# A decode step of attention with a gated feed-forward: the gate's weights in nine DMAs, V's last tiles in pieces, the last head of wo in 21 parts

## Chip, cores and metric

The kernel runs on one core of one Trainium2 chip. The metric is device time in microseconds (us), median of three runs; lower is better.

## The reference, cut to what matters

```
q = x @ wq                                    # x [1,512], wq [512, 32*128], 32 heads of 128
scores = q . k_cache * 128**-0.5              # k_cache [32, 65536, 128] bf16
p = softmax(scores);  o = p @ v_cache         # v_cache [32, 65536, 128] bf16
a = o.reshape(1, 4096) @ wo                   # wo [4096, 512]
b = (silu(x @ w_gate) * (x @ w_up)) @ w_down  # 512 -> 1792 -> 512
g = sigmoid((x * gate_w).sum())               # gate_w [512]
out = g * a + (1 - g) * b
```

One token attends to 65536 keys in each of 32 heads. K and V together are 1 GiB, each byte is read once, and everything else is small beside them.

## The kernel before, in words

Each head's K and V are cut into G = 4 tiles of 128 partitions x 128 rows x 128 elements (4 MB), so that N = 128 K tiles and 128 V tiles are loaded. All of them, and the large weights, pass through a ring of five slots of 4 MB (`take`, `give`). A load is issued by SyncE (SP) and waits until its slot has been given back by the last reader.

For a K tile, VectorE multiplies by the query and adds halves (`products`), TensorE sums the rest over column groups into PSUM (`scores`), and VectorE folds the result (`fold`). After the fourth tile of a head the softmax follows (`row_max`, `exponentials`). For a V tile, `values` issues 32 matmuls, each of which takes four of the tile's 128 row groups. After a head's fourth V tile, `head_out` copies the sums from PSUM (for the last head ScalarE and VectorE take half each), turns them into a column `oT`, and `project(h)` multiplies that by the head's 128 rows of wo and adds to `a_ps`.

The order is written out by hand: a list of steps (n, v), where n is the K tile and v the V tile of the step. At the end there are steps with V tiles alone. Each engine works through its instructions in this order.

The transfers that the change touches:

- At the start ScalarE's queue (ACT) issues `xT` (L91) and `gwT` (L92), and SP issues `wq_first`, then K tiles 0, 1 and 2 (`load_k`, L107), the rest of wq (L121) and K tile 3. `gwT` is first read by `gate_sum` (L190), after the second K tile's products.
- `load_v` cuts only the last V tile, at 64, 96 and 112 of its 128 row groups. Each piece is a DMA of its own, so that `values` can begin on a piece when that piece has landed.
- wo for heads 0 to 15 comes in groups of four heads. The last 16 heads (LATE = 16) are kept unprojected until the end. Their 2 MB of wo come into a ring slot by `load_late` (L166), after the last V tile, in four DMAs of 6, 5, 4 and 1 heads. After `head_out(H - 1)` come 16 calls of `project` and then the output.

All DMAs of SP and ACT take eight completion semaphores in turn, in the order of the program. In the built program, a DMA that takes a semaphore again first waits on its issuing queue until the DMA eight places earlier has landed. So at most eight DMAs are under way, whatever their size.

Of the kernel before, what the change touches and what calls it, by code (L numbers as in the profile page):

```python
# [11 lines left out]
P = 128  # L12
# [3 lines left out]
NB = 128  # L16
# [10 lines left out]
LATE = 16  # L27
# [3 lines left out]
def kernel(  # L31
# [14 lines left out]
    nc = tc.nc  # L46
# [3 lines left out]
    _, H, Sk, Dh = A_k_cache.shape  # L50
    D = A_x.shape[2]
    F = B_w_gate.shape[1]
    KT = D // P
# [3 lines left out]
    N = H * G  # L57
# [6 lines left out]
    small = ctx.enter_context(tc.tile_pool(name="small", bufs=2))  # L64
# [13 lines left out]
    def take(name):  # L78
        slot = free.pop(0)
        held[name] = slot  # L80
        return ring.tile(
            [P, NB * Dh], bf16, name=name.split(".")[0], tag=f"slot{slot}"
        )

    def give(name):
        free.append(held.pop(name))

    xT = consts.tile([P, KT], bf16, name="xT")
    gwT = consts.tile([P, KT], bf16, name="gwT")
    with nc.allow_non_contiguous_dma(reason="small"):  # L90
        nc.scalar.dma_start(out=xT, in_=A_x[0, 0, :].rearrange("(p t) -> p t", t=KT))  # L91
        nc.scalar.dma_start(out=gwT, in_=gate_w.rearrange("(p t) -> p t", t=KT))  # L92

    QW = QG * Dh
    wq_rows = A_wq.rearrange("(p t) f -> p t f", t=KT)
# [3 lines left out]
    K_tiles, V_tiles, S_tiles, F_tiles, P_tiles, O_tiles = {}, {}, {}, {}, {}, {}  # L99

    def load(dst, cache, n, name, cuts=(0, NB)):
        h, g = divmod(n, G)
        t = take(f"{name}.{n}")
        view = t.rearrange("p (j d) -> p j d", d=Dh)
        src = cache[0, h, g * NB * P : (g + 1) * NB * P, :].rearrange("(p j) d -> p j d", j=NB)
        for a, b in zip(cuts[:-1], cuts[1:]):
            nc.sync.dma_start(out=view[:, a:b, :], in_=src[:, a:b, :])  # L107
        dst[n] = view

    def load_k(n):  # L110
        load(K_tiles, A_k_cache, n, "K_t")

    def load_v(n):
        load(V_tiles, A_v_cache, n, "V_t", (0, NB) if n < N - 1 else (0, 64, 96, 112, NB))

    load_k(0)
    load_k(1)
    load_k(2)
    wq_t = take("wq_t.0")
    wq_rest = wq_t[:, : KT * (H * Dh - QW)].rearrange("p (t f) -> p t f", t=KT)  # L120
# [36 lines left out]
    def load_wo(g):  # L157
        wo_tiles[g] = wo_pool.tile([P, WG, D], bf16, name="wo_sb", tag="wo_sb")
        rows = A_wo[g * WG * P : (g + 1) * WG * P, :]
        nc.sync.dma_start(out=wo_tiles[g], in_=rows.rearrange("(h p) n -> p h n", p=P))  # L160

    def load_late(cuts):
        late = take("wo_late.0")[:, : LATE * D].rearrange("p (h n) -> p h n", n=D)
        rows = A_wo[(H - LATE) * P :, :].rearrange("(h p) n -> p h n", p=P)
        for a, b in zip(cuts[:-1], cuts[1:]):
            nc.sync.dma_start(out=late[:, a:b, :], in_=rows[:, a:b, :])  # L166
        return late

    def feed_forward_in():
# [41 lines left out]
    def feed_forward_mid(gu_sb, eg):  # L211
        nc.vector.tensor_scalar_add(eg, eg, 1.0)
        nc.vector.reciprocal(eg, eg)
        hprod = consts.tile([P, FT], f32, name="hprod")
        nc.vector.tensor_tensor(out=hprod, in0=gu_sb[:, :FT], in1=eg, op=ALU.mult)
        hT = consts.tile([P, FT], bf16, name="hT")
        nc.vector.tensor_tensor(out=hT, in0=hprod, in1=gu_sb[:, FT:], op=ALU.mult)
        return hT
# [13 lines left out]
    def products(n, a=0, b=NB):  # L232
        h = n // G
        K = K_tiles[n][:, a:b, :]
        qb = q_bc[:, h * Dh : (h + 1) * Dh]
        q_rep = bass.AP(
            tensor=qb.tensor,
            offset=qb.offset,
            ap=[list(qb.ap[0]), [0, b - a], [1, Dh]],
        )  # L240
        yield nc.vector.tensor_tensor(out=K, in0=K, in1=q_rep, op=ALU.mult)  # L241
        half = Dh
        while half > width_of(n):
            half //= 2
            yield nc.vector.tensor_tensor(  # L245
                out=K[:, :, 0:half], in0=K[:, :, 0:half], in1=K[:, :, half : 2 * half],
                op=ALU.add,
            )
# [15 lines left out]
    def fold(n):  # L264
        h, g = divmod(n, G)
        if g == 0:
            S_tiles[h] = small.tile([P, NBH], f32, name="S_sb")
        nc.vector.tensor_reduce(  # L268
            out=S_tiles[h][:, g * NB : (g + 1) * NB], in_=F_tiles.pop(n), axis=AXIS.X, op=ALU.add
        )  # L270

    def row_max(h):
        m = small.tile([P, 1], f32, name="m")
        nc.vector.tensor_reduce(out=m, in_=S_tiles[h], axis=AXIS.X, op=ALU.max)  # L274
        diag = small.tile([P, P], f32, name="diag")
        nc.scalar.activation(out=diag, in_=ident_f, func=ACT.Copy, scale=m)  # L276
        mT_ps = psum_m.tile([P, P], f32, name="mT_ps", tag="misc")
        nc.tensor.matmul(mT_ps, lhsT=ones_f, rhs=diag, start=True, stop=True)  # L278
        return mT_ps

    def exponentials(h, mT_ps):
        top = small.tile([P, 1], f32, name="top")
        nc.vector.tensor_reduce(out=top, in_=mT_ps, axis=AXIS.X, op=ALU.max)  # L283
        bias = small.tile([P, 1], f32, name="bias")
        nc.scalar.activation(out=bias, in_=top, func=ACT.Copy, scale=-scale)  # L285
        P_tiles[h] = ppool.tile([P, NBH], bf16, name="P_sb")
        nc.scalar.activation(  # L287
            out=P_tiles[h], in_=S_tiles[h], func=ACT.Exp, bias=bias, scale=scale,
            accum_out=rowsum[:, h : h + 1],
        )  # L290
        del S_tiles[h]
# [26 lines left out]
    def head_out(h, last=False):  # L318
        O_sb = small.tile([4, 4 * Dh], f32, name="O_sb")
        O_ps = O_tiles.pop(h)  # L320
        cut = 2 * Dh if last else 4 * Dh
        nc.scalar.activation(out=O_sb[:, :cut], in_=O_ps[:, :cut], func=ACT.Copy)  # L322
        if last:
            nc.vector.tensor_copy(out=O_sb[:, cut:], in_=O_ps[:, cut:])  # L324
        oh_ps = psum_m.tile([P, 1], f32, name="oh_ps", tag="misc")
        for c in range(4):
            nc.tensor.matmul(  # L327
                oh_ps,
                lhsT=O_sb[:, c * Dh : (c + 1) * Dh],
                rhs=ident_f[0:4, c : c + 1],  # L330
                start=(c == 0),
                stop=(c == 3),
            )
        nc.scalar.activation(  # L334
            out=oT[:, h : h + 1], in_=oh_ps, func=ACT.Copy, scale=rg[:, h : h + 1]
        )

    def project(h):
        rows = wo_tiles[h // WG][:, h % WG, :] if h < H - LATE else wo_late[:, h - (H - LATE), :]
        nc.tensor.matmul(  # L340
            a_ps, lhsT=oT[:, h : h + 1], rhs=rows, start=False, stop=(h == H - 1)
        )
# [27 lines left out]
    rest = gate_value(eg2)  # L370
    scores(2)
    load_v(0)
    ff = feed_forward_in()
    give("gu_t.0")
# [14 lines left out]
    for n, v in steps:  # L389
        if n is not None and n > G:  # L390
            load_k(n)
        if v is not None:
            if v % (WG * G) == 2 and v // (WG * G) < (H - LATE) // WG:
                load_wo(v // (WG * G))
            if v:
                load_v(v)
            if v == N - 1:
                wo_late = load_late((0, 6, 11, 15, LATE))
        vector = iter(()) if n is None else products(n)
        top_of = None  # L400
        if n is None:
            top_of = H - 1 if F_tiles else None
        elif n % G == 0:
            top_of = n // G - 1
            vector = (i for a in (0, NB // 2) for i in products(n, a, a + NB // 2))
        if top_of is not None:
            next(vector, None)
            fold(top_of * G + G - 1)
            mT_ps = row_max(top_of)
            next(vector, None)  # L410
            exponentials(top_of, mT_ps)
        if n == G:
            hT = feed_forward_mid(*ff)
        for _ in vector:
            pass
        if n is not None and n % G:
            fold(n - 1)
        if tot_ps is not None:
            weight(*tot_ps)
            tot_ps = None  # L420
        if n == G:
            feed_forward_out(hT, rest)
            give("wd_t.0")
        if done is not None:
            head_out(done)
        if v is not None:
            values(v)
        if top_of is not None:
            tot_ps = top_of, total(top_of)
        if n is not None:  # L430
            scores(n)
        if done is not None and done < H - LATE:
            project(done)
        done = v // G if v is not None and v % G == G - 1 else None
    head_out(H - 1, last=True)
    for h in range(H - LATE, H):
        project(h)

    out_sb = consts.tile([1, D], bf16, name="out_sb")
# [34 lines left out]
```

## Time and profile before

| | |
|---|---|
| time, median of 3 runs | 2543.21 us (2543.02 to 2543.95) |
| the profiled execution's own time | 2543.14 us |
| its span, first to last instruction | 2541.4 us |
| bytes moved by DMA | 1088.48 MB, mean 428 GB/s |
| VectorE busy | 2083.7 us (82%) |
| TensorE matmuls busy | 1528.2 us (60%) |

The span is what the profile's views divide up; 1.7 us of the execution's time lie outside it. Times in the views count from the span's first instruction. "Landing" is the moment at which all of a DMA's completion counts have arrived. "SPq" is SP's instruction queue, which issues most of the DMAs; the duration of an issue is how long it held the queue.

### The profile page before, as it was taken

To read this page: it belongs to the slowest core of one execution; us is meant where nothing else is said; L and a number is where in the kernel's file an instruction comes from. 1 tells how busy PE (TensorE), PEld (TensorE's weight loads), DVE (VectorE), ACT (ScalarE), POOL (GpSimd) and SP (SyncE) were. 2 spreads that over 40 slices of the span, in tenths; PEclk is the share of its full clock that TensorE was granted. 3 is DMA by queue.
4 is the path that set the end of the run, shared out by engine and by line. 5 is a ranking of instruction groups with operands and counts; after the bars stand their busy time and mean duration, and the time that the engine had idled before them with its cause. 6 is when DMAs were issued, how large, how long until landed. Compare 5 with 4: busy or idle time off the path is not lost.

```text
span 2541.4 us, 13067 instructions
## 1 busy us (share of the span) xinstructions
PE 1528.2 (60%) x5730; PEld 577.4 (23%) x5730; DVE 2083.7 (82%) x745; ACT 77.3 (3%) x207; POOL 0.7 (0%) x6
## 2 busy tenths in 40 slices
PE   4566566665666555556665565566556655665568
PEld 2222122221222212212222222222122222222223
DVE  7888888788878999988888888888888888888850
ACT  1000000000000000000000000000000000000000
POOL 0000000000000000000000000000000000000000
PEclk9777777777777777787777777777777777777779
DMA  9999999999999999999999999999999999999998
GB/s 412 427 433 431 429 433 429 433 430 431 432 430 431 430 432 432 430 429 432 431 432 430 432 432 429 431 433 430 430 433 431 429 434 431 430 432 432 430 431 341
DMA packets 43354, 1088.48 MB, mean 428 GB/s; under 512 B 4641, under 2 KB 9250, under 8 KB 10018
## 3 DMA queue, kind: packets, MB, share of 16 engines
q1 hardware_dynamic: 43010, 1087.65, 99.7%
q8 instruction: 44, 0.72, 0.1%
q14 instruction: 12, 0.10, 0.0%
q10 hardware_dynamic: 288, 0.00, 0.0%
HBM read 1087.64 MB, written 0.00 MB: 428 GB/s over the span
## 4 chain that ended last, share of the span: by engine, by line
DMA 71%; PE 23%; DVE 6%; issue 0%; ACT 0%; SPq 0%; DVEq 0%; ACTq 0%
DMA V_t<-in_A_v_cache_dram 65%; PE O_ps L308 21%; DMA K_t<-in_A_k_cache_dram 6%; DVE K_t L241 3%; DVE K_t L245 2%; PE S_ps L254 1%; DVE S_sb L268 0%; PE oh_ps L327 0%; PE a_ps L340 0%; DVE m L274 0%; ACT P_sb L287 0%; ACT O_sb L322 0%; PE mT_ps L278 0%; DVE top L283 0%; ACT diag L276 0%
## 5 line engine op out<-in xcount | busy, mean ns | idle before, releaser
L308 PE MATMUL O_ps<-V_t,P_sb 128*4 128x512 bf16 x4096 | 1156.5, 452 | 680.6 <-DMA V_t<-in_A_v_cache_dram 680.6
L241 DVE TENSOR_TENSOR K_t<-K_t,q_bc 128x16384 bf16<-128x16384 bf16 (+1 forms) x159 | 1117.1, 7026 | 363.1 <-DMA K_t<-in_A_k_cache_dram 363.1
L245 DVE TENSOR_TENSOR K_t<-K_t 128x8192 bf16<-128x8192 bf16 (+1 forms) x314 | 859.6, 2738 | 8.6
L308 PEld LDWEIGHTS <-P_sb 128*4 128x4 bf16 x4096 | 393.6, 97 | 1424.7 <-issue 1083.6
L254 PE MATMUL S_ps<-K_t,ident_b 128*128 128x512 bf16 x1056 | 263.9, 393 | 98.4 <-DVE K_t L245 98.3
L254 PEld LDWEIGHTS <-ident_b 128*128 128x128 bf16 x1056 | 98.0, 101 | 245.8 <-issue 156.0
L278 PE MATMUL mT_ps<-diag,ones_f 128*128 128x128 f32 x64 | 24.3, 481 | 148.7 <-ACT diag L276 148.7
L327 PE MATMUL oh_ps<-ident_f,O_sb 4*128 4x1 f32 x256 | 55.5, 334 | 74.4 <-ACT O_sb L322 74.4
L268 DVE TENSOR_REDUCE S_sb<-S_ps 128x128 f32<-128x512 f32 x128 | 87.4, 682 | 4.6 <-PE S_ps L254 4.6
L276 ACT ACTIVATE diag<-ident_f,m 128x128 f32<-128x128 f32 x32 | 12.9, 402 | 2128.7 <-DVE m L274 2128.7
L327 PEld LDWEIGHTS oh_ps<-ident_f,O_sb 4*128 4x128 f32 x256 | 52.8, 301 | 84.5 <-ACT O_sb L322 80.1
L278 PEld LDWEIGHTS mT_ps<-diag,ones_f 128*128 128x128 f32 x64 | 15.2, 295 | 165.8 <-ACT diag L276 165.8
L324 DVE COPY O_sb<-O_ps 4x256 f32<-4x256 f32 x1 | 0.4, 411 | 55.8 <-ACT O_sb L322 55.8
L287 ACT ACTIVATE P_sb<-S_sb,bias 128x512 bf16<-128x512 f32 x32 | 23.1, 722 | 1.0
L274 DVE TENSOR_REDUCE m<-S_sb 128x1 f32<-128x512 f32 x32 | 21.9, 686 | 1.1
L322 ACT ACTIVATE O_sb<-O_ps 4x512 f32<-4x512 f32 (+1 forms) x32 | 18.1, 566 | 136.5 <-PE O_ps L308 136.5
L300 DVE RECIPROCAL recip<-tot_ps 128x1 f32<-128x1 f32 x32 | 5.0, 156 | 12.8 <-PE tot_ps L295 12.8
L295 PEld LDWEIGHTS tot_ps<-rowsum,ones_f 128*128 128x128 f32 x64 | 9.5, 188 | 14.0 <-issue 14.0
L295 PE MATMUL tot_ps<-rowsum,ones_f 128*128 128x1 f32 x64 | 12.2, 260 | 0.0
L334 ACT ACTIVATE oT<-oh_ps,rg 128x1 bf16<-128x1 f32 x32 | 8.4, 264 | 63.0 <-PE oh_ps L327 63.0
L283 DVE TENSOR_REDUCE top<-mT_ps 128x1 f32<-128x128 f32 x32 | 9.1, 283 | 1.0 <-PE mT_ps L278 1.0
L285 ACT ACTIVATE bias<-top 128x1 f32<-128x1 f32 x32 | 6.5, 203 | 62.8 <-DVE top L283 62.8
(42 smaller groups left out, 69.0 us busy)
## 6 DMA issues: line engine op xcount, KB each, us to landing
K_t<-in_A_k_cache_dram SPq DMA_DIRECT2D x128, 4096.0 KB, 37.2
V_t<-in_A_v_cache_dram SPq DMA_DIRECT2D x127, 4096.0 KB, 29.6
wq_t<-in_A_wq_dram SPq DMA_DIRECT2D x1, 3584.0 KB, 40.1
wo_sb<-in_A_wo_dram SPq DMA_DIRECT2D x4, 512.0 KB, 30.6
V_t<-in_A_v_cache_dram SPq DMA_DIRECT2D x1, 2048.0 KB
gu_t<-in_B_w_gate_dram SPq DMA_DIRECT2D x1, 1792.0 KB, 23.7
gu_t<-in_B_w_up_dram SPq DMA_DIRECT2D x1, 1792.0 KB, 27.6
wd_t<-in_B_w_down_dram SPq DMA_DIRECT2D x1, 1792.0 KB, 23.6
```

What stands on the lines that cost most here:

```text
L241: yield nc.vector.tensor_tensor(out=K, in0=K, in1=q_rep, op=ALU.mult)
L245: yield nc.vector.tensor_tensor(out=K[:, :, 0:half], in0=K[:, :, 0:half], in1=K[:, :, half : 2 * half], op=ALU.add,)
L254: nc.tensor.matmul(S, lhsT=ident_b, rhs=K_tiles[n][:, :, c : c + QUAD], start=(c == 0), stop=(c == width - QUAD),)
L268: nc.vector.tensor_reduce(out=S_tiles[h][:, g * NB : (g + 1) * NB], in_=F_tiles.pop(n), axis=AXIS.X, op=ALU.add)
L274: nc.vector.tensor_reduce(out=m, in_=S_tiles[h], axis=AXIS.X, op=ALU.max)
L276: nc.scalar.activation(out=diag, in_=ident_f, func=ACT.Copy, scale=m)
L278: nc.tensor.matmul(mT_ps, lhsT=ones_f, rhs=diag, start=True, stop=True)
L287: nc.scalar.activation(out=P_tiles[h], in_=S_tiles[h], func=ACT.Exp, bias=bias, scale=scale, accum_out=rowsum[:, h : h + 1],)
L295: nc.tensor.matmul(tot_ps, lhsT=ones_f, rhs=rowsum[:, h : h + 1], start=True, stop=True)
L308: nc.tensor.matmul(O_tiles[h], lhsT=P_tiles[h][:, g * NB + j : g * NB + j + 4], rhs=V_tiles[n][:, j : j + 4, :], start=(g == 0 and j == 0) ...
L322: nc.scalar.activation(out=O_sb[:, :cut], in_=O_ps[:, :cut], func=ACT.Copy)
L327: nc.tensor.matmul(oh_ps, lhsT=O_sb[:, c * Dh : (c + 1) * Dh], rhs=ident_f[0:4, c : c + 1], start=(c == 0), stop=(c == 3),)
```

## The change

- `gwT` is no longer issued by ACT beside `xT`. SP issues it between K tiles 1 and 2: eight DMAs of eight partitions each (64 bytes per DMA) and one of the other 64 partitions.
- V tiles N-3 and N-2 (125 and 126) come in two halves each. The last V tile's cuts stay.
- `load_late` takes the 16 heads as 3, 5, 5, 2 and 1. The one head at the end is cut by partitions: one DMA of 64, four of 8, four of 4, four of 2 and eight of 1, which is 21 DMAs for 128 KB in place of one.
- In the last `head_out`, three `project` calls stand between the copies out of PSUM and the matmuls that turn the sums; the other 13 follow as before.

The order of all other work, the matmuls' number and shape, and the arithmetic stay as they were. The total of DMAs on the two queues grows from 274 to 305.

```diff
-        nc.scalar.dma_start(out=gwT, in_=gate_w.rearrange("(p t) -> p t", t=KT))
...
     def load_v(n):
-        load(V_tiles, A_v_cache, n, "V_t", (0, NB) if n < N - 1 else (0, 64, 96, 112, NB))
+        cuts = {N - 3: (0, 64, NB), N - 2: (0, 64, NB), N - 1: (0, 64, 96, 112, NB)}
+        load(V_tiles, A_v_cache, n, "V_t", cuts.get(n, (0, NB)))
 
     load_k(0)
     load_k(1)
+    gw_rows = gate_w.rearrange("(p t) -> p t", t=KT)
+    with nc.allow_non_contiguous_dma(reason="small"):
+        for a in range(0, P // 2, 8):
+            nc.sync.dma_start(out=gwT[a : a + 8], in_=gw_rows[a : a + 8])
+        nc.sync.dma_start(out=gwT[P // 2 :], in_=gw_rows[P // 2 :])
     load_k(2)
...
-    def load_late(cuts):
+    def load_late(cuts, parts):
...
         for a, b in zip(cuts[:-1], cuts[1:]):
-            nc.sync.dma_start(out=late[:, a:b, :], in_=rows[:, a:b, :])
+            if b < LATE:
+                nc.sync.dma_start(out=late[:, a:b, :], in_=rows[:, a:b, :])
+                continue
+            first = 0
+            for size, count in parts:
+                for _ in range(count):
+                    part = slice(first, first + size)
+                    nc.sync.dma_start(out=late[part, a:b, :], in_=rows[part, a:b, :])
+                    first += size
...
         if last:
             nc.vector.tensor_copy(out=O_sb[:, cut:], in_=O_ps[:, cut:])
+            for early in range(H - LATE, H - LATE + 3):
+                project(early)
...
-                wo_late = load_late((0, 6, 11, 15, LATE))
+                wo_late = load_late((0, 3, 8, 13, 15, LATE), ((64, 1), (8, 4), (4, 4), (2, 4), (1, 8)))
...
     head_out(H - 1, last=True)
-    for h in range(H - LATE, H):
+    for h in range(H - LATE + 3, H):
         project(h)
```

## The prediction

> **What bounds the kernel now.** I read the page's queues and chain first, then the chain of waits and SP's issues at the two ends of the kernel, where the change lies.
>
> ```profile
> q1 hardware_dynamic: 43010, 1087.65, 99.7%
> DMA 71%; PE 23%; DVE 6%; issue 0%; ACT 0%; SPq 0%; DVEq 0%; ACTq 0%
> ```
>
> The first line is SP's queue: its packets fill 99.7% of the time of all 16 DMA engines over the whole span. No engine is as full (VectorE 82%), so a stretch in which the DMA engines stand still is never made up later, and a faster compute engine brings nothing until the data end. Only the last few microseconds, after the bulk has landed, belong to others. The chain from 2484 us, in order of time (start, duration, what):
>
> ```profile
> 2484.56 34.64 DMA V_t<-in_A_v_cache_dram
> 2519.21 0.04 issue
> 2519.25 13.99 PE O_ps L308 x64
> ...
> 2533.32 0.38 ACT O_sb L322
> 2533.71 0.04 issue
> 2533.75 1.05 PE oh_ps L327 x8
> 2534.80 3.56 PE a_ps L340 x16
> ```
>
> V tile 126 lands at 2519.2, TensorE then does tiles 126 and 127 without a pause (64 matmuls, 0.219 us each), turns the sums and projects 16 heads (0.223 us each) until 2538.36. The copies, the output DMA and the end take 3.0 us more.
>
> SP's issues, at the start and at the end, and the landings of two of them:
>
> ```profile
> 1.46 1.55 SPq L107 DMA_DIRECT2D K_t<-in_A_k_cache_dram  x3
> 3.05 0.72 SPq L121 DMA_DIRECT2D wq_t<-in_A_wq_dram  x1
> 3.81 0.73 SPq L107 DMA_DIRECT2D K_t<-in_A_k_cache_dram  x1
> ```
>
> ```profile
> 2491.47 1.75 SPq L107 DMA_DIRECT2D V_t<-in_A_v_cache_dram  x4
> 2498.38 30.34 SPq L166 DMA_DIRECT2D wo_late<-in_A_wo_dram  x4
> 2539.22 0.33 SPq L443 DMA_DIRECT2D out_dram<-out_sb  x1
> ```
>
> ```profile
> K_t<-in_A_k_cache_dram SPq DMA_DIRECT2D x1, 4096.0 KB, 22.4
> ```
>
> ```profile
> wo_late<-in_A_wo_dram SPq DMA_DIRECT2D x1, 128.0 KB, 8.1
> ```
>
> The third fence is K tile 1 alone, issued at 2.12: it lands at 24.5 us. K tile 2 was issued right behind it, long before, so the engines pass from one to the next. The last fence is wo's last head, issued at 2526.76, landed at 2534.85: all bulk data are in by then. The four V pieces show the price of one issue in an unbroken row: 1.75 us for four, of which the last holds 0.43, so 0.44 to 0.47 from one start to the next; an issue that stands alone, as out's, holds 0.33.
>
> **The start: gwT.** The eight semaphores decide here. In the program's order xT has the first, wq_first the second, K tiles 0 and 1 the third and fourth; the nine gwT DMAs take the fifth to eighth, then the first to fourth again, then the fifth. So gwT's seventh DMA waits on SP for K tile 0, and the eighth for K tile 1, which lands at 24.5. Behind it in SP's queue stand gwT's ninth DMA, K tile 2, the rest of wq and K tile 3. The queue of the engines is empty when K tile 1 has ended. K tile 2 is then issued at 24.55 + 0.37 + 0.47 = 25.4 instead of 2.58.
>
> How long do the engines stand still? K tiles follow each other by 9.7 us (K tile 2 lands at 34.2 before). From an issue to the landing of something tiny: out is issued at 2539.22, and SP's wait for its landing ends at 2540.4, 1.2 us; xT needs 1.8. A 4 MB tile from empty engines therefore lands about 1.2 to 1.8 us plus 9.7 after its issue: 25.4 + 10.9 to 11.5 = 36.3 to 36.9, or 2.1 to 2.7 us later than before. Take 2.4. Below nothing is excluded, since the bytes behind are the same. The cover that could hide it would be queued transfers, and there are none: everything later on SP stands behind the waiting issue. VectorE's need of K tile 2 is at 41.9, so it does not stall at once, but every later tile lands 2.4 us later and the queue is full from then on: +2.4 us at the end. The gate's consumer at 41.65 isn't reached by this. ACT loses one issue of 0.46 that nothing waited for. The DMA count before K tile 2 grows by eight, one full turn, so all later waits on semaphores pair the same tiles as before; the steady part stays.
>
> **V's halves and the early projections.** Each half is 2 MB. Before, cutting the last tile into four made its landings 9.93 us apart in all against 9.72 for a whole one, so the two cuts cost some 0.1 us. In exchange TensorE can take tile 126's first half about 4.9 us before 2519.2. It then follows the landings: with tile 127's last piece in at 2529.2 it ends near 2531.1 instead of 2533.2. Three projections (0.67 us) go where TensorE idled 0.5 us. If nothing else bound the end, the last projection would start near 2535.4 instead of 2537.98: -2.5 us.
>
> **wo's last head.** It does bind. Bulk data end as before: 15 heads of wo take 15/16 of the 5.7 us from V's last landing (2529.14) to 2534.85, so they land at 2530.3, 2532.1, 2533.9 and 2534.6 for 3, 5, 5 and 2 heads, and the part of 64 rows at 2534.8. Each small part waits for the DMA eight before: the fourth one behind the 64 rows for the 3 heads, the next three for the landings at 2532.1, 2533.9 and 2534.6, the ninth of the 21 for the part of 64 rows. So SP issues the ninth at about 2535.1, and twelve more in a row: 12 x 0.47 = 5.6, the last at 2540.7. It lands 1.2 later, at 2541.9. Project of head 31 needs all 21 parts and starts then instead of at 2537.98: +3.9 us, and everything gained on TensorE is idle time before it. For the pitch the nearest rows are the V pieces in an unbroken row (0.47); the other end is the 0.33 + 0.04 of an issue that stands alone, which gives 2540.7 and +2.7. Upward the longest issue that wasn't blocked by a full queue holds 0.73, which gives +7.5. The copy, output and end follow as before.
>
> The Trainium skill (DMA: Bandwidth & Descriptors, section "Anatomy of one DMA") puts the fixed price of one DMA at about 2.0 us; by that the last part would land 0.8 later and the time be 2550.2. The row of out, 1.2 us, is this kernel's and disagrees. Its section "Why a DMA increments its semaphore by 16 and not by 1" says that for a DMA on fewer than 16 DMA engines the issuing sequencer writes the missing counts itself. Out's row, one partition, holds SP no longer than a whole V tile (0.33 both), so I charge nothing for it.
>
> **Sum.** 2.4 + 3.9 = 6.3 (the 0.1 for the cuts stands in the landings above). On the profiled execution's 2543.14 that is 2549.4, 0.24% over the median of 2543.21. What a measurement of this kernel can tell from no change is about 0.2%, 5.1 us, so the bounds are 2538.1 and 2548.3.
>
> **Rivals.** *Not slower: the parts hide.* If the small parts are issued at about 0.1 us each, or SP doesn't wait for each turn of eight, the last part lands with the bulk, and TensorE's -2.5 shows: 2543.1 with the stall at the start, 2540.7 without. The point from which it decides: twelve issues must take under 0.6 us in place of 5.6. Against it stand the V pieces' rows. 0.12. *One half is missing.* The stall at the start is covered, or K tile 1's landing doesn't hold SP: 2547.0. For it speaks only that gwT is 1 KB; against it, the order of semaphores. 0.10. *Dearer parts.* Issues of one to eight partitions hold SP 0.73 each, as K tile 3's did at the start: 12 x 0.30 more, 2553.0. Against it out's 0.33. 0.14. The forecast keeps 0.64, with 2547.5 to 2552 as its own range: 2.1 to 2.7 at the start and 2.7 to 6 at the end.
>
> **Chances and range.** Faster by more than 0.2% would need -5.1 us; parts and stall both free give -2.5, so 0.02. Slower: nine tenths of the forecast, the dearer parts and a little of the missing half, 0.75. Within 0.2%: 0.23, the rest. The range leaves out most of the hidden parts and reaches to dearer ones: 2545.5 to 2554.
>
> **What would show it.** In the profile after: K tile 2's issue at about 25.4 rather than 2.58, a hole of 2 to 2.7 us in the DMA rate near 25, K tile 2 landing near 36.6; steady landings 9.7 apart; V's 64 last matmuls broken by waits for pieces and ended about 2 us earlier against the data; some 13 issues of wo's parts in an unbroken row after the bulk has landed, and project of head 31 waiting for them 4 to 6 us. Wrong would be: no hole near 25 us, parts issued under 0.2 us apart, or the chain's last DMA being a V piece or wo's first heads.

## The result and the profile after

The changed kernel takes 2548.34 us (median of 16 runs, 2548.05 to 2549.72); the kernel before, run beside it, 2543.30 us. That is 5.04 us more, a ratio of 1.0019 (95% interval 1.0012 to 1.0026). The profiled execution's span is 2546.1 us against 2541.4.

The lines that answer to those of before. SP's DMA queue and the shares of the chain, from the page after:

```profile
q1 hardware_dynamic: 43586, 1087.66, 99.5%
DMA 73%; PE 22%; DVE 4%; SPq 1%; issue 0%; ACT 0%
```

The bytes are the same, but the packets no longer fill 99.7% of the span, and SP's own queue now has a share of the chain that ended last: 17.7 us, of which 11.1 are one issue of wo's rows, at 2517.20. That issue costs next to nothing: wo's 15 heads have landed 5.5 us after V's last piece, and 5.4 us after it in a kernel shown below (the changes at the end alone) whose chain has no such issue. Why an issue can hold SP for so long is not shown. What costs, the two ends show. SP's issues at the start (start, time that the issues of the row span, what):

```profile
1.49 1.08 SPq L106 DMA_DIRECT2D K_t<-in_A_k_cache_dram  x2
2.61 21.70 SPq L121 DMA_DIRECT2D gwT<-in_gate_w_dram  x8
24.35 0.51 SPq L122 DMA_DIRECT2D gwT<-in_gate_w_dram  x1
24.91 0.59 SPq L106 DMA_DIRECT2D K_t<-in_A_k_cache_dram  x1
```

The reader is to see 21.70: eight DMAs of 64 bytes span the whole time in which two K tiles flow. K tile 2 is issued at 24.91, in place of 2.58. The waits of SP in the first 60 us name what it waited for (us in total, times, longest):

```profile
SPq L121 <- DMA K_t<-in_A_k_cache_dram: 18.9, 2, 9.4
```

The DMA engines meanwhile, one microsecond each from 23 to 27 (the last two columns are the share of their time and GB/s):

```profile
23.00:24.00 1.00, 0.00 (x0) 0.00 (x0) 0.97 (x2) 0.00 (x0) 0.00 (x0) 1.00 0.07 1
24.00:25.00 1.00, 0.00 (x0) 0.00 (x0) 1.00 (x1) 0.00 (x0) 0.00 (x0) 1.00 0.01 0
25.00:26.00 1.00, 0.00 (x0) 0.00 (x0) 1.00 (x1) 0.00 (x0) 0.00 (x0) 1.00 0.04 1
26.00:27.00 1.00, 0.00 (x0) 0.00 (x0) 1.00 (x1) 0.00 (x0) 0.00 (x0) 1.00 1.66 459
```

A packet counts where it starts, so the first of these microseconds still holds the rest of packets begun before 23. From 24 to 26 nothing flows but a part of gwT's few bytes. In the kernel before, the same two microseconds are:

```profile
24.00:25.00 1.00, 0.00 (x0) 0.00 (x0) 1.00 (x1) 0.00 (x0) 0.00 (x0) 1.00 0.76 328
25.00:26.00 1.00, 0.00 (x0) 0.00 (x0) 1.00 (x1) 0.00 (x0) 0.00 (x0) 1.00 0.76 328
```

K tile 2's last completion count comes at 37.3 instead of 34.2. The end, from the chain in order of time:

```profile
2517.20 11.13 SPq L172
...
2537.55 0.25 SPq L178
2537.80 0.04 issue
2537.85 0.29 SPq L178
...
2541.13 0.25 SPq L178
2541.38 0.05 issue
2541.43 1.26 DMA wo_late<-in_A_wo_dram
2542.70 0.04 issue
2542.74 0.39 PE a_ps L355
```

From 2537.55 to 2541.43 the chain is SP issuing one part after the other, then 1.26 us until the last lands, then head 31's projection. TensorE from V tile 126's second half on:

```profile
2522.14 3.61 PE L321 MATMUL O_ps<-V_t,P_sb 128*4 128x512 bf16 x16 [1.30 <-DMA V_t<-in_A_v_cache_dram]
2527.04 7.07 PE L321 MATMUL O_ps<-V_t,P_sb 128*4 128x512 bf16 x32 [1.29 <-DMA V_t<-in_A_v_cache_dram]
2533.94 0.81 PE L355 MATMUL a_ps<-wo_late,oT 128*1 128x512 bf16 x3
2534.68 1.05 PE L342 MATMUL oh_ps<-ident_f,O_sb 4*128 4x1 f32 x8
2535.66 2.94 PE L355 MATMUL a_ps<-wo_late,oT 128*1 128x512 bf16 x12
2542.74 0.38 PE L355 MATMUL a_ps<-wo_late,oT 128*1 128x512 bf16 x1 [4.14 <-DMA wo_late<-in_A_wo_dram]
```

TensorE has 15 of the 16 projections done at 2538.6 and then idles 4.14 us for the last part.

### The profile page after: what moved, and what is told of

Its sections match the earlier page's. It is cut to its first block, busy times and chain, and to the rows that moved or that the text cites. A ratio compares the mean times of both kernels' runs of the same rounds, so it can differ in the third digit from the quotient of the medians.

```text
span 2546.1 us, 13106 instructions
## 1 busy us (share of the span) xinstructions
PE 1530.1 (60%) x5730; PEld 577.7 (23%) x5730; DVE 2084.1 (82%) x745; ACT 77.3 (3%) x207; POOL 0.7 (0%) x6
## 4 chain that ended last, share of the span: by engine, by line
DMA 73%; PE 22%; DVE 4%; SPq 1%; issue 0%; ACT 0%
DMA V_t<-in_A_v_cache_dram 65%; PE O_ps L321 21%; DMA K_t<-in_A_k_cache_dram 8%; DVE K_t L254 2%; DVE K_t L258 1%; PE S_ps L267 1%; SPq L172 0%; DMA wo_late<-in_A_wo_dram 0%; DVE S_sb L281 0%; PE oh_ps L342 0%; DVE m L287 0%; SPq L178 0%; ACT P_sb L300 0%; SPq L106 0%; PE mT_ps L291 0%
```

## The experiments

Theory A says that two independent losses add up: a hole in the DMA stream at 25 us, made by the turn of eight completion semaphores, and a row of issues at the end that cannot begin until the bulk has landed and holds SP once per part. The first four kernels take the two ends apart, the next four vary the parts, the last two split what the change gains. Each was timed beside the kernel before (medians of before: 2543.18, 2543.19 and 2543.09 in the three groups).

**gwT's nine DMAs alone**, put into the kernel before:

```diff
-        nc.scalar.dma_start(out=gwT, in_=gate_w.rearrange("(p t) -> p t", t=KT))
...
     load_k(1)
+    gw_rows = gate_w.rearrange("(p t) -> p t", t=KT)
+    with nc.allow_non_contiguous_dma(reason="small"):
+        cuts = (*range(0, 65, 8), 128)
+        for a, z in zip(cuts[:-1], cuts[1:]):
+            nc.sync.dma_start(out=gwT[a:z], in_=gw_rows[a:z])
     load_k(2)
```

> The kernel before with gwT's nine DMAs alone; the end is as before. Theory A (each issue waits for the DMA eight places earlier, so K tile 2 is issued only when K tile 1 has landed, and the DMA engines stand still): K tile 2 lands 3.1 us later, as in the changed kernel (37.3 against 34.2), and all of it is left at the end: 2543.3 + 2.9 = 2546.2. Rival B (the hole at 25 us is made up by the queue later, and the whole 5.0 comes from wo's 21 parts): 2543.3.

Measured: 2546.61 us, 3.43 more (ratio 1.0012, 1.0003 to 1.0021). The hole is not made up later, so rival B falls. The loss is 0.5 us above the 2.9 that A gave.

**Six DMAs in the same place**, cuts 0, 16, 32, 48, 64, 96, 128:

> The kernel before with gwT in six DMAs on SP at the same place (four of 16 and two of 32 partitions). Theory A: K tile 2 now stands eight places behind K tile 0, which lands at 14.3, while K tile 1 still flows for 9.7 us; no hole, 2543.3. Rival C (the small DMAs on SP ahead of K tile 2 are dear in themselves, each its share of the 2.9): 6/9 x 2.9 = 1.9 more, 2545.2.

Measured: 2543.11 us, 0.07 less than before (0.9999, 0.9991 to 1.0008).

**Seven DMAs**, cuts 0, 16, 32, 48, 64, 80, 96, 128:

> As with six, but seven DMAs (six of 16 and one of 32 partitions): one small DMA more. Theory A: K tile 2 itself now waits for K tile 1's landing at 24.0; it is issued 0.9 us sooner than with nine (24.05 against 24.91), so the hole is 2.9 - 0.9 = 2.0: 2545.3. Rival C: 7/9 x 2.9 = 2.3 more, 2545.6, but with six at 2545.2 beside it, a step of 0.3 in place of 2.0.

Measured: 2545.59 us, 2.41 more (1.0008, 0.9999 to 1.0017). The seventh DMA costs 2.5 us and the six before it nothing, which rival C has no way to give. The interval by itself reaches to no change, but the single runs of the two kernels do not meet: the slowest with six DMAs took 2544.48, the fastest with seven 2544.72. Nine DMAs cost 1.0 more than seven; K tile 2 is issued 0.7 us later there, at 25.27 against 24.58. The traces show the step as A describes it. With six, SP's issues and the DMA rate:

```profile
2.58 2.83 SPq L121 DMA_DIRECT2D gwT<-in_gate_w_dram  x6
14.62 0.35 SPq L106 DMA_DIRECT2D K_t<-in_A_k_cache_dram  x1
24.40 0.55 SPq L125 DMA_DIRECT2D wq_t<-in_A_wq_dram  x1
```

```profile
24.00:25.00 1.00, 0.00 (x0) 0.00 (x0) 1.00 (x1) 0.00 (x0) 0.00 (x0) 1.00 1.26 459
```

K tile 2 waits too, but for K tile 0, at a time when K tile 1 still flows. With seven it waits for the one before it:

```profile
24.58 0.35 SPq L106 DMA_DIRECT2D K_t<-in_A_k_cache_dram  x1
```

```profile
24.00:25.00 1.00, 0.00 (x0) 0.00 (x0) 1.00 (x1) 0.00 (x0) 0.00 (x0) 1.00 0.03 0
```

So it is neither the bytes nor the number of small DMAs that costs, but what stands eight places ahead of the next large one.

**The changes at the end alone:** gwT back on ACT in one DMA.

> The changed kernel with gwT back on ACT in one DMA; V's halves, the early projections and wo's 21 parts stay. Theory A: the start is as before, and the end is what the changed kernel's is less the hole: project of head 31 at 2542.74 - 2.88 = 2539.86 instead of 2537.98, 2543.3 + 1.9 = 2545.2. Rival B: 2548.3. Rival D (the parts are hidden behind the bulk, and the start is all): 2540.8.

Measured: 2545.08 us, 1.90 more (1.0007, 0.9998 to 1.0016), against 1.9 expected. The two ends alone sum to 3.43 + 1.90 = 5.33, and the whole change is 5.04; the difference is within the intervals. This run's interval reaches to no change, but the 2548.3 of rival B and the 2540.8 of rival D both lie outside it: they fall.

**The last head in one DMA**, the rest as in the kernel just shown:

```diff
-                wo_late = load_late((0, 3, 8, 13, 15, LATE), ((64, 1), (8, 4), (4, 4), (2, 4), (1, 8)))
+                wo_late = load_late((0, 3, 8, 13, 15, LATE), ((128, 1),))
```

> As tail_only, but wo's last head comes in one DMA of 128 partitions. Theory A (the last issues in a row, 0.295 us each, hold the end): head 31's rows land with the bulk near 2534.9, TensorE bounds the end, and the 13 projections start the last at about 2535.5 instead of 2537.98: 2543.3 - 2.5 = 2540.8. Rival E (V's halves and the early projections bring nothing, the landing of the bulk decides): 2543.3.

Measured: 2540.70 us, 2.49 less than before (0.9989, 0.9980 to 0.9998). This is the lowest median of the study, and rival E falls. Its chain at the end:

```profile
2524.45 7.07 PE O_ps L317 x32
2531.51 0.65 PE a_ps L351 x3
2532.16 0.98 PE oh_ps L338 x8
2533.14 2.91 PE a_ps L351 x13
```

No DMA of wo stands in it: TensorE goes from the first piece of V's last tile to the last projection without a pause.

**Nine parts:** `((64, 1), (8, 8))`, otherwise as with the changes at the end alone.

> As tail_only, but the last head in 9 parts (one of 64 partitions, eight of 8): twelve issues fewer, and the last part still waits for the part of 64. Theory A (price by the number of issues behind the bulk's landing): 12 x 0.295 = 3.5 less, 2545.2 - 3.5 = 2541.7. Rival F (the price is the one wait for the part of 64 rows to land, whatever follows): 2545.2.

Measured: 2542.13 us, 2.95 less than with 21 parts, where A gave 3.5 (to before 0.9994, 0.9985 to 1.0003). Rival F falls; A's slope was a little too steep here. Its chain after the ninth part's issue:

```profile
2534.83 1.53 DMA wo_late<-in_A_wo_dram
2536.36 0.46 issue
```

The last part lands 1.53 us after its issue, and 0.46 more pass until the projection starts. Both together are 0.7 us more than with 21 parts, which A's sum doesn't have. No issue follows the ninth here, and the time is still 1.43 us above the kernel with the last head in one DMA: the wait for the bulk, one more issue and its landing are a price of their own.

**37 parts:** `((64, 1), (8, 4), (1, 32))`.

> As tail_only, but the last head in 37 parts (64, four of 8, 32 of 1): 16 issues more, the same bytes. Theory A: 16 x 0.295 = 4.7 more than tail_only, 2549.9. Rival G (the turn of eight decides: each eight more parts cost a full issue and landing, 1.26 + 0.3): 2 x 1.6 = 3.1 more, 2548.3. Rival F: 2545.2.

Measured: 2549.99 us (to before 1.0025, 1.0016 to 1.0035), 4.91 more than with 21 parts, for the same bytes: 4.91 / 16 = 0.31 us per part, close to the issue pitch of 0.295 us (from one start to the next in the row). Rival G, a full turn for each eight parts, would give 3.1; it falls, and so does F.

**The losses without the gains:** the changed kernel without V's halves and the early projections.

> The changed kernel without V's halves and without the early projections; gwT's nine DMAs and wo's 21 parts stay. Theory A (TensorE's gain at the end is idle time before the last part): the same as the changed kernel, 2548.3. Rival H (the gain is real and only smaller than the loss): 2.5 more, 2550.8.

Measured: 2548.37 us (1.0019, 1.0010 to 1.0028), the same as the changed kernel's 2548.34. Its last projection:

```profile
2542.85 0.38 PE L353 MATMUL a_ps<-wo_late,oT 128*1 128x512 bf16 x1 [1.85 <-DMA wo_late<-in_A_wo_dram]
```

Before it TensorE idles 1.85 us; in the changed kernel it idles 4.14. What V's halves and the early projections give is idle time. Rival H falls.

**Only the halves,** from the kernel with the last head in one DMA, all 16 projections after the turned sums:

> As whole_head, but the 16 projections all follow the turned sums, as before; only V's halves and wo's other cuts stay. Theory A: TensorE ends V's matmuls near 2531.2 in place of 2533.2 and has 16 projections to do, so 2.0 of the 2.5 us stay: 2541.2. Rival I (the halves bring nothing because tile 127 lands no sooner; the early projections bring it): 2543.2.

Measured: 2541.21 us, 1.88 less than before (0.9991, 0.9982 to 1.0000), where rival I gave no gain: it falls.

**Only the early projections,** from the same kernel, V tiles 125 and 126 whole:

> As whole_head, but V tiles 125 and 126 come whole; the early projections and wo's other cuts stay. Theory A: three projections (0.67 us) fill the 0.5 us in which TensorE waited for the copies: 2543.2 - 0.5 = 2542.7. Rival I: 2540.7.

Measured: 2542.62 us, 0.47 less (0.9999, 0.9990 to 1.0008). The medians of 1.88 and 0.47 make 2.35 of the 2.49 that both give together, as A has it. The 1.88 are clear by the single runs (2541.03 to 2541.45, and never under 2542.61 before); the 0.47 are not told apart from no change. wo's cuts at 3, 8, 13 and 15 heads stand in all these kernels, and no run shows what they do alone.

## Why the prediction held, step by step

**What bounds the kernel** held. The DMA engines are the bound, and a hole in their stream at 25 us is still there at 2522: V tile 126's second half releases TensorE at 2522.1, against 2519.2 for the whole tile before.

**The start** held in its mechanism to the issue: the seventh and the eighth small DMA wait for K tiles 0 and 1, K tile 2 is issued at 24.91 (forecast 25.4; the 0.5 us between are K tile 1's, which landed at 24.0 in place of 24.5). The term was too small: 2.4 us, where the profile after shows 3.1 at K tile 2's landing and 2.9 at V tile 126, and gwT's nine DMAs alone cost 3.43. What was mis-sized is the time from K tile 2's issue to its landing on empty engines: 10.9 to 11.5 us forecast, 12.4 measured. The kernel with seven DMAs, in which K tile 2 is issued 0.02 us after K tile 1 has landed, shows nearly the same:

```profile
K_t<-in_A_k_cache_dram SPq DMA_DIRECT2D x1, 4096.0 KB, 12.3
```

I had taken the landing time of a tiny DMA for the whole price of an empty stream. The packet records of the changed kernel show what was left out: K tile 2's first sixteen packets start 1.2 to 2.3 us after the issue, and twelve of them take 1.7 to 2.2 us, where a packet of this size takes 1.21 in the flowing stream. Why they are slow stays open. The engines had run dry; but gwT's small DMAs also complete as late as 25.7 with seven and 26.3 in the changed kernel, when these packets have just begun. With six, where the stream never stops, the second sixteen packets of K tile 2 run while small DMAs complete, and they take 1.2 to 1.8 us too.

**V's halves and the early projections** held: -2.5 forecast if nothing else bound the end, -2.49 measured with the last head in one DMA. That they vanish behind the parts held too.

**wo's last head** held in its mechanism: the row of issues begins behind the bulk, the ninth at 2537.85, where the forecast 2535.1 and the shift of 2.9 from the start give 2538.0. The term was too large: 3.9 us forecast, 1.90 measured with the changes at the end alone. What was mis-sized is the pitch of 0.47 us, taken from the row of V pieces. The last twelve issues of the chain hold SP 0.25 us each and start 0.295 apart, so from the ninth issue to the last 3.6 us pass instead of 5.6. That is about the whole error of the term. The row that I had put at the other end of the range (an issue that stands alone) gave +2.7 and was nearer, though still too dear. The last part lands 1.26 us after its issue, near out's 1.2, which the sum had used. The 2.0 us for one DMA that the prediction set beside it (the Trainium skill, DMA: Bandwidth & Descriptors, "Anatomy of one DMA") are given in that section as a fit for DMAs that GpSimd issues. GpSimd issues no DMA in these kernels, so no run here shows that figure, and for SP's parts the 1.26 us are what counts.

**The sum.** 6.3 was forecast, 5.04 measured: half to one microsecond too little at the start, two too much at the end. That the total lies near is in part luck of opposite signs: the start cost about a fifth to two fifths more than its term, the end half of its term. The forecast's own range is written from 2547.5, but its lowest terms, 2.1 and 2.7, give 2547.9; the result lies inside it either way. Against the prediction's line between no change and slower, 0.2%, the measured 5.04 us are 0.198%, and the interval (0.12 to 0.26%) holds both sides. So the result does not tell whether the 0.75 for slower or the 0.23 for no clear change was the better call.

Of the **rivals**, the one in which the parts hide falls: twelve issues took 3.6 us. The point that the prediction gave for it, twelve issues in under 0.6 us, was wrong in its own terms. Its 0.1 us each make 1.2, and even with no issue behind the ninth the last part would land at 2535.1 + 1.2 = 2536.3, after TensorE's 2535.4. The kernel with nine parts has no issue behind the ninth, and there head 31's projection starts at 2536.82, against 2535.66 with one DMA. A missing half is excluded by the runs of each end alone. Dearer parts are excluded by the pitch.

## What to carry to other kernels

Where DMAs share a few completion semaphores in turn, count what stands eight places ahead of each large load: a handful of tiny DMAs between two tiles can make the next tile's issue wait until the tile before it has landed, and where the DMA engines bound the kernel that hole stays to the end. At the end of a kernel, data that the last step needs should come in as few DMAs as the split allows: behind the bulk, each further one costs an issue, and the last of them costs its landing too. Before costing an end, ask which of the last steps truly waits: here cutting V's tiles and moving projections up was worth 2.5 us, and all of it was hidden by 128 KB in 21 pieces.

## What the runs showed of the hardware that I had not expected

In unbroken rows, issues on SP cost less where fewer partitions are addressed, whatever the bytes. DMAs of one and two partitions start 0.295 us apart, those of eight 0.33, and those of 16 and 32 partitions 0.48 (six of them in 2.83 us, the last holding 0.42), as much as V's last pieces of 128 partitions. The gwT DMAs of 16 partitions carry 128 bytes and those pieces 0.5 to 1 MB, so size is not what sets it. The number of partitions is not all either: out, which is one partition in every kernel, holds SP 0.33 us in the kernel before and 0.24 behind the 21 parts. What sets the price is not shown.

A hole costs more than the time between the last landing and the next issue. With seven DMAs that time is 0.02 us, and K tile 2 lands 2.6 us later than in the kernel before (36.87 against 34.23).

A landing late in this kernel is far from its first completion count. In the kernel before, K tile 2's sixteen counts arrive within 0.5 us of each other, those of V tile 126, near the end, within 9.6. From 2520 to 2525 the DMA engines are busy 0.83 of their time and from 2530 to 2535 only 0.41, which looks as if some of them had finished well before the others. Neither the prediction nor any run asks why, though 9.6 us are more than everything that this change gained or lost.
